# Two attentions, forward and backward, in one kernel: token-stage groups reordered, stage-edge loads and tiles moved, memory projections cut into three pieces

## The chip, the cores and the metric

The kernel runs on one core of one Trainium2 chip. The metric is device time of one execution in microseconds (us). A core has TensorE (PE in the profile; PEld is its weight load), VectorE (DVE), ScalarE (ACT), GpSimd (POOL) and SyncE (SP, which here only issues DMAs). All engines work at once, each through its own list of instructions in order, and they wait for one another by semaphores.

## The reference

A plain attention A with one shared key and value head, a recurrent attention B that carries eight memory rows from segment to segment, a gate that mixes them, and the gradients of everything with respect to the inputs and weights:

```python
def _A_ref(x, wq, wk, wv, wo):            # x 1x2048x576, 32 heads of 18, one k and one v for all heads
    q = (x @ wq).reshape(B, S, H, Dh).transpose(0, 2, 1, 3)
    k, v = x @ wk, x @ wv
    p = softmax(einsum('bhqd,bkd->bhqk', q, k) * Dh ** -0.5)
    return einsum('bhqk,bkd->bhqd', p, v).transpose(0, 2, 1, 3).reshape(B, S, H * Dh) @ wo

def _B_ref(x, mem0, Wq, Wk, Wv, Wo, seg_len):   # 32 heads of 128, segments of 32 rows, 8 memory rows
    mask = (idx[:, None] < M) | (idx[:, None] >= idx[None, :])
    mem = mem0
    for s in range(n_seg):                      # 64 segments, one after the other
        h = concatenate([mem, x[:, s * seg_len:(s + 1) * seg_len]], axis=1)
        q, k, v = (einsum('btd,dhe->bhte', h, W) for W in (Wq, Wk, Wv))
        p = softmax(where(mask, einsum('bhqe,bhke->bhqk', q, k) * scale, -1e9))
        o = einsum('bhte,hed->btd', einsum('bhqk,bhke->bhqe', p, v), Wo)
        mem = o[:, :M]
        outs.append(o[:, M:])
    return concatenate(outs, axis=1)

g = sigmoid((x * gate_w).sum(-1, keepdims=True))
out = g * _A_ref(x, ...) + (1 - g) * _B_ref(x, mem0, ...)
# returned: out, and by vjp the gradients of x, wq, wk, wv, wo, mem0, Wq, Wk, Wv, Wo, gate_w
```

All inputs and outputs are bf16.

## The kernel before

The program is a sequence of stages on one core. B is recurrent, so its forward and its backward pass are chains of small steps over the 64 segments; A is attention over 2048 x 2048 for 32 heads, a large sweep of equal steps with no dependence between them. The kernel weaves the two: a generator for a chain and a generator for a sweep are advanced in turn by `weave`, so that the sweep's matmuls fill the chain's waits.

In order of time: preparation; `b_proj` (projections of all tokens of B); `b_chain_fwd` woven with `a_pass1` (A's forward); the token stage `b_bulk`; `b_chain_bwd` woven with `a_pass2` (A's backward); `b_post` (the token gradients that the chain left over, and their product with the weights); `b_dw` (weight gradients of B, woven with the last 96 of the 1024 sweep steps of `a_pass2` and with `mem_tok`, which lays memory gradients out by tokens); `a_final`.

**Token stage, `b_bulk`.** 128 groups of (128 tokens, 4 heads) pass through a software pipeline. One turn of its loop is a tick; in each tick the list `order` names the steps and by how many ticks each lags behind the first: scores of one group, the softmax of an older one, output of one still older. `st_QT`, `st_KT`, `st_OT`, `st_VT`, `st_GT` transpose q, k, o, v and dO on TensorE into the PSUM tile `x_tr`, which has two buffers; QT and KT carry a fifth transpose along (x_dS, x_P), whose copies are `x_DT` and `x_PT`. `st_Om` and `st_Qm` open an accumulation in `x_po` (two buffers) with the whole array (memory part), `st_Ox` and `st_Qx` close it in 32 x 32 tiles (token part), and ScalarE copies it out (L740, x_o and x_dq). `B_(i)` are quarters of the output projection. `st_R` and `st_M` are softmax on VectorE and GpSimd. ScalarE also copies `x_oT` (L867) and `x_vT`.

**Woven backward chain.** `b_chain_bwd` yields 14 times in a segment, so it has 14 pieces, and between two pieces `weave` runs one step of `a_pass2`: scores `b_S` (one buffer of two banks), their exponential `b_E` on ScalarE (L1893), `b_dP`, the product `b_dS` on VectorE (L1918), and two products into `b_acc`. `lead` (12) sweep steps run ahead of the first piece, `extra` adds some after pieces 4, 7 and 9 of the first segment, and `early` (`load_WT`) asks for one twelfth of the weights WT at every fourth step, ahead of the sweep step, whose DMAs are on the same SP queue.

A segment goes, in pieces p0 to p13:

- p0, p1: `proj_part`, the gradient of the memory rows (`dm`) times `WoT`, for the two halves of the heads into PSUM tiles `r_pj` and `r_x` (one buffer each), each 5 blocks (`NKT`) of 4 matmuls, copied to `r_dOm` by ScalarE (`evac`).
- p2: `mem_T` (transposes, in r_x), copy `r_dOT` on ScalarE, `r_prod` on GpSimd, four DMAs of dOm issued by GpSimd, and the first `mem_grad` in r_pj.
- p3: `r_x` for dP, then `r_dS` on VectorE and `r_dSB` (`expand`) on GpSimd.
- p4 to p12: `heads(n)`, 48 units per segment of 4 matmuls `r_pj<-WT,r_dT`, in portions of 2, 8, 4, 4, 3, 8, 8, 6, 5; between them two more `mem_grad`, `pad_in` (GpSimd copies dS into a padded tile) and `pad_T` (VectorE transposes it, `r_dsq`), loads for the next segment, and `kv_mm(n)` in r_x with its copy and store `kv_out(n)` one piece later, which are token gradients of k and v that have nothing to do with the recurrence. `kv_first(s)` gives the numbers n0 of a segment: none in the first 4 and the last 4 segments, otherwise 3 or 4 of them.
- p13: sums of rows, the next `dm`, and a last `kv_mm`.

Sweep, chain and token gradients share the in-order lists: ScalarE holds exponentials and all copies, GpSimd holds small products and the issue of all stores, VectorE holds b_dS and the transposes.

**Stage edges.** Tiles live in pools that open and close as a stack, so a pool of one stage lies where an earlier stage had another, and its first loads wait until the old tiles are read. For the woven chain the pools are opened as rw (WoT), a3s (b_QS), a3k (b_KV), rs (the chain's tiles). `b_post` takes its tiles from rotating names of pool `sp`, `b_dw` then opens wA, whose `w_d` tiles are loaded from SP, half by plain DMAs and half by DMA transposes (L1425); `mem_tok` loads `z_src` on SP too (L588).

Of the kernel before, what the change touches and what calls it, by code (L numbers as in the profile page):

```python
# [50 lines left out]
class Kern:  # L51
# [227 lines left out]
    def weave(self, chain, sweep, lead, extra=(), early=None, n_early=0):  # L279
        steps = itertools.count()  # L280

        def step():
            i = next(steps)
            if i % 4 == 0 and i // 4 < n_early:
                early(i // 4)
            next(sweep, None)

        for _ in range(lead):
            step()
        extra = dict(extra)  # L290
        for i, _ in enumerate(chain):
            for _ in range(1 + extra.get(i, 0)):
                step()
        for _ in sweep:
            pass
# [287 lines left out]
    def mem_tok(self, wi, sp, psum):  # L583
        nc = self.nc

        def load(mt):
            src = sp.tile([P, 16, 256], BF16, name="z_src", bufs=2)
            nc.sync.dma_start(src[:], self.dTm_dram[mt][:, wi])  # L588
            return src
# [68 lines left out]
    def b_bulk(self, wp, lp, sp, psum):  # L658
# [243 lines left out]
        def st_K(t):  # L902
# [12 lines left out]
            if t % 4 == 3:  # L915
                c2 = t // 4 % 2
                for i in range(4):
# [3 lines left out]
        B_ = lambda i: lambda t: st_B(t, i)  # L921
        order = [(None, st_QT), (7, B_(0)), (None, st_KT), (7, B_(1)), (4, st_Om), (5, st_OT), (7, B_(2)), (5, st_VT),
                 (7, B_(3)), (None, st_SDm), (0, st_GT), (9, st_Qm), (2, st_R), (7, st_K),
                 (None, st_SDx), (1, st_M), (4, st_Ox), (9, st_Qx)]
        done = {st_Ox: (4,), st_VT: (5,), st_SDx: (6,), st_K: (7,), st_Qx: (9,)}
# [67 lines left out]
    def b_chain_bwd(self, wot, sp, kd, kvp, keep, psum):  # L993
# [119 lines left out]
        for s in reversed(range(NSEG)):  # L1113
# [6 lines left out]
            dOm = sp.tile([P, 8, E], BF16, name="r_dOm", bufs=1)  # L1120
            for j, nm in enumerate(("r_pj", "r_x")):
                pj = psum.tile([P, 512], F32, name=nm, bufs=1)
                self.proj_part(pj, d_, self.WoT, j, range(NKT))
                self.evac(dOm[:, 4 * j:4 * j + 4, :].rearrange("p u e -> p (u e)"), pj[:], use="s")
                if j == 1:
                    x_rows(s, 0, pT[:, 0, :])
                yield
            src = self.mem_T(dOm, psum, "r_x", 1)
# [56 lines left out]

            heads(2)
            kv_mm(n0)
            pad_in("ds", dS[:, 1, :])
            if s:
                load_a(s - 1, nxt)  # L1190
            yield
            kv_out(n0)
            heads(8)
            dSq = pad_T("ds")
            dSqB = blocks(dSq, "r_dSqB")
            x_rows(s, 1, dS[:, 0, :])
            yield
            heads(4)
            mem_cols(0, mem_grad("r_x", ((rows(L["kx"]), blk(dSB)), (rows(mrow["k"]), blk(dSB, 8)))))
            yield  # L1200
            mem_cols(1, mem_grad("r_x", ((rows(mrow["dx"]), [perm] * 8), (rows(mrow["q"]), blk(dSqB)))))
            heads(4)
            if s:
                load_b(s - 1, nxt)
            nc.gpsimd.dma_start(self.dTm_dram[s // 16][:, :, s % 16, :], dTc[:].rearrange("p w u c t -> p w (u c t)"))
            yield
            load_dT(s - 1, 2)
            heads(3)
            kv_mm(n0 + 1)
            yield  # L1210
            kv_out(n0 + 1)
            heads(8)
            if s:
# [9 lines left out]
            load_dT(s - 1, 0)  # L1223
            heads(6)
            if n1 - n0 == 4:
# [4 lines left out]
            if n1 - n0 == 4:  # L1230
                kv_out(n0 + 2)
            heads(5)
            hp = sp.tile([64, 2 * GD], F32, name="r_hp", tag="r_dSB", bufs=1)
# [38 lines left out]
    def b_post(self, sp, rp, psum, wH):  # L1272
# [5 lines left out]
        NC = NG // 2  # L1278
        pdx, C, sB, mR, T_ = {}, {}, {}, {}, {}

        def load_s(n):
# [11 lines left out]
        def load(c, names):  # L1293
# [6 lines left out]
            for w in names:  # L1300
# [5 lines left out]
                if w == "pd":  # L1306
                    d[w] = rp.tile([P, 2, 8, SEG], BF16, name="y_pd", bufs=3)
                    nc.sync.dma_start(d[w][:], self.pd_dram[tt][:, :, h0:h0 + 8, :])
                    continue
                d[w] = (rp if w == "q" else sp).tile([P, 8, P], BF16, name=f"y_{w}", bufs=3)  # L1310
                if w == "dq":
# [5 lines left out]
        def st_KV(t):  # L1317
# [13 lines left out]
            for w, pk in zip(("dk", "dv"), pks):  # L1331
                if t % 2 == 0:
                    d[w] = sp.tile([P, 8, P], BF16, name=f"y_t{w}", bufs=2)
                nc.scalar.copy(d[w][:, r, :], pk[:])
                if t % 2 == 1:
                    h0 = 8 * (t // 2 % 4)
                    nc.gpsimd.dma_start(self.xtok[w][tt * P:(tt + 1) * P, h0 * P:h0 * P + 1024],
                                      d[w][:].rearrange("p h e -> p (h e)"))

        def st_T(t):  # L1340
            d = C[t // 2]
            T_[t] = {"dq": d["dq"][:, 4 * (t % 2):4 * (t % 2) + 4, :]}
            for w in ("dk", "dv"):
                pt = psum.tile([P, 4, P], BF16, name="y_pt", bufs=2)
                for i in range(4):
                    self.tr(pt[:, i, :], d[w][:, 4 * (t % 2) + i, :], P)
                T_[t][w] = sp.tile([P, 4, P], BF16, name="y_T", bufs=5)
                nc.vector.tensor_copy(T_[t][w][:], pt[:])
            if t % 2 == 1:
                C.pop(t // 2)  # L1350
# [17 lines left out]
        stages = (st_KV, st_T, st_H)  # L1368
        dxt = [sp.tile([P, D], BF16, name=f"y_dx{i}") for i in range(2)]
        load(0, ("pd", "q", "dO"))  # L1370
# [678 lines left out]
def build_full(tc, A_x, A_wq, A_wk, A_wv, A_wo, B_mem0, B_Wq, B_Wk, B_Wv, B_Wo, gate_w, grad_out, outs_raw,  # L2049
# [10 lines left out]
    with SB("const") as cpool, tc.tile_pool(name="dram", bufs=1, space=bass.MemoryType.DRAM) as dram:  # L2060
# [18 lines left out]
        with ExitStack() as man:  # L2079
# [39 lines left out]
            k.alloc_WT(twp)  # L2119
            with SB("rw") as rw, SB("a3s") as a3s, SB("a3k") as a3k, SB("rs") as rs, \  # L2120
                    SB("rk") as rk, SB("rv") as rv, SB("rd") as rd, PS("rp") as rp, PS("a3p") as a3p:
# [88 lines left out]
```

## Time and profile before

| what | value |
|---|---|
| time, median of 3 runs | 5476.64 us (5473.39 to 5486.16) |
| profiled execution | 5478.13 us, its span 5476.4 us (1.7 us lie outside) |
| TensorE busy | 5171.7 us, 94% |
| VectorE, ScalarE, GpSimd busy | 65%, 60%, 40% |
| mean granted TensorE clock | 0.981 of full speed |
| HBM traffic | 522 MB read, 371 MB written |

| stretch of the span (us) | stage | TensorE busy | ScalarE busy | granted clock |
|---|---|---|---|---|
| 431 to 2143 | forward chain with A's forward | 1644.00 | 1360.27 | 0.99 |
| 2143 to 2783 | token stage | 576.94 | 359.04 | 0.97 |
| 2783 to 2873 | lead steps, first segment begins | 56.22 | 47.40 | 0.62 |
| 2873 to 4374 | backward chain with A's backward | 1429.58 | 1152.33 | 1.00 |
| 4392 to 4605 | b_post | 211.94 | 46.67 | 1.00 |
| 4605 to 4643 | edge to b_dw | 21.62 | 9.18 | 0.71 |
| 4643 to 5373 | b_dw | 727.64 | 156.69 | 1.00 |

How to read the profile: one execution was recorded by the hardware. A row of a timeline has start, duration, engine, source line (L740 is line 740 of the kernel), operation, output tile and input tiles, shapes, and a count where several alike follow each other; brackets give how long the engine was idle just before and which instruction or DMA released it. SPq is SP issuing DMAs. A group of the page or of the lines view adds up all such rows of one line and tile pair: busy time, mean in ns, and the idle time before them with its releasers. One group is not one limit: what ends a stage has to be read in that stage.

### The profile page before, as it was taken

What the parts mean: (1) busy time and instruction counts of PE and PEld (TensorE: products, weight loads), DVE (VectorE), ACT (ScalarE), POOL (GpSimd) and SP (SyncE); (2) the same over time, 40 slices, a digit from 0 to 9 for tenths busy, and PEclk for the clock granted to TensorE, in tenths of its full rate; (3) what the DMA queues carried; (4) which work ended last, traced back from release to release, by engine and by line L of the source; (5) the groups of instructions that cost most, each with busy time, mean ns of one, the idle gap of its engine ahead of it and who ended that gap; (6) DMA issues with size and microseconds to landing.
All of it is one profiled execution on the core that took longest, in us unless ns stands there. A gap on an engine that the chain in (4) does not pass through costs nothing. (4 is left out here: it accounts for less than half of the span.)

```text
span 5476.4 us, 221351 instructions
## 1 busy us (share of the span) xinstructions
PE 5171.7 (94%) x95713; PEld 2805.1 (51%) x95713; DVE 3579.9 (65%) x7083; ACT 3306.7 (60%) x4738; POOL 2163.2 (40%) x4186
## 2 busy tenths in 40 slices
PE   7999999999999998999979999999999998999998
PEld 6434444444444444766635555555555476754444
DVE  5337888888888887666658778888788822333322
ACT  4327787777777886655557777777777722222211
POOL 4004554555555544433324455455445411121113
PEclk9999999999999999999979999999999999999999
DMA  6645776666676555888874788888888878956553
GB/s 216 222 173 130 138 138 130 131 135 130 133 134 121 112 111 144 259 250 248 255 243 128 184 181 184 181 185 183 180 184 184 160 201 213 255 187 205 182 165 108
DMA packets 1048630, 959.14 MB, mean 175 GB/s; under 512 B 598882, under 2 KB 896747, under 8 KB 1038050
## 3 DMA queue, kind: packets, MB, share of 16 engines
q1 hardware_dynamic: 938434, 687.66, 54.2%
q0 software_dynamic: 100784, 247.24, 14.8%
q8 instruction: 748, 12.26, 1.0%
q10 hardware_dynamic: 8432, 10.08, 0.6%
q14 instruction: 232, 1.90, 0.1%
HBM read 522.08 MB, written 371.33 MB: 163 GB/s over the span
## 5 line engine op out<-in xcount | busy, mean ns | idle before, releaser
L1918 DVE TENSOR_TENSOR b_dS<-b_dP,b_E 128x512 bf16<-128x512 f32 x2048 | 1315.4, 684 | 533.5 <-PE b_dP L86 246.0
L1779 DVE TENSOR_TENSOR a_W<-a_dP,a_E 128x512 bf16<-128x512 f32 x2048 | 1315.7, 685 | 288.0 <-issue 131.3
L1893 ACT ACTIVATE b_E<-b_S 128x1024 bf16<-128x1024 f32 x1024 | 1048.8, 1024 | 605.2 <-PE b_dP L86 505.4
L1749 ACT ACTIVATE a_E<-a_S 128x1024 bf16<-128x1024 f32 x1024 | 1049.9, 1025 | 260.9 <-PE a_dP L86 173.4
L86 PEld LDWEIGHTS <-b_QS 32*128 32x128 bf16 (+1 forms) x8192 | 235.5, 89 | 564.0 <-issue 512.3
L86 PE MATMUL b_S<-b_KV,b_QS 32*128 32x512 bf16 x2048 | 408.7, 392 | 91.5 <-ACT b_E L1893 67.3
L86 PE MATMUL r_pj<-WT,r_dT 128*32 128x288 bf16 x12288 | 488.6, 289 | 6.0 <-issue 5.8
L86 PE MATMUL w_acc<-w_d,w_h 128*128 128x512 bf16 (+1 forms) x2400 | 484.6, 380 | 0.0
L86 PE MATMUL a_S<-a_QD,l_KV 32*128 32x512 bf16 x2048 | 400.6, 385 | 38.0 <-ACT a_E L1749 33.2
L86 PE MATMUL b_acc<-b_dS,b_QS 128*18 128x512 bf16 x2048 | 420.5, 392 | 3.2 <-issue 2.4
L86 PE MATMUL a_acc<-a_W,l_WK 128*32 128x512 bf16 x4096 | 413.8, 391 | 0.3 <-DVE a_W L1779 0.2
L86 PE MATMUL a_acc<-a_E,l_VK 128*32 128x512 bf16 x4096 | 404.7, 381 | 7.2 <-issue 2.7
L86 PE MATMUL b_dP<-b_KV,b_QS 32*128 32x512 bf16 x2048 | 409.2, 394 | 1.3 <-DVE b_dS L1918 1.3
L86 PE MATMUL b_acc<-b_E,b_QS 128*18 128x512 bf16 x2048 | 405.9, 392 | 2.1 <-issue 2.1
L86 PE MATMUL a_dP<-a_QD,l_KV 32*128 32x512 bf16 x2048 | 399.7, 386 | 0.5 <-issue 0.5
L86 PEld LDWEIGHTS <-r_dT 128*32 128x32 bf16 x12288 | 323.9, 97 | 101.2 <-issue 13.8
L86 PEld LDWEIGHTS <-w_h 128*128 128x128 bf16 (+1 forms) x2688 | 224.9, 100 | 257.9 <-issue 20.9
L86 PEld LDWEIGHTS <-hm 128*32 128x32 bf16 x7680 | 203.7, 97 | 195.7 <-issue 1.4
L870 POOL TENSOR_TENSOR x_prod<-x_dOT,x_oT 128x512 bf16<-128x512 bf16 x128 | 148.0, 1157 | 296.8 <-ACT x_oT L867 274.2
L86 PEld LDWEIGHTS <-l_KV 32*128 32x128 bf16 x4096 | 121.6, 91 | 250.1 <-issue 205.5
L86 PEld LDWEIGHTS <-l_WK 128*32 128x32 bf16 x4096 | 106.7, 93 | 222.0 <-issue 221.7
L86 PE MATMUL x_b<-WoN,x_oT 128*128 128x288 bf16 x1024 | 212.6, 291 | 3.2 <-issue 3.2
(465 smaller groups left out, 10106.7 us busy)
## 6 DMA issues: line engine op xcount, KB each, us to landing
b_QS<-qs_dram SPq DMA_DIRECT2D x232, 200.0 KB
dOx_dram<-p_tok SPq DMA_DIRECT2D x16, 1024.0 KB
c_vx<-vx_dram SPq DMA_DIRECT2D x64, 256.0 KB
krow_dram<-c_k POOLq DMA_DIRECT2D x64, 256.0 KB, 5.2
qrow_dram<-c_q POOLq DMA_DIRECT2D x64, 256.0 KB, 3.9
vrow_dram<-c_v POOLq DMA_DIRECT2D x64, 256.0 KB
x_q<-qx_dram SPq DMA_DIRECT2D x32, 512.0 KB
x_dO<-dOx_dram SPq DMA_DIRECT2D x32, 512.0 KB
```

Source lines behind the costliest of these rows:

```text
L86: return self.nc.tensor.matmul(out, lhsT, rhs, start=start, stop=stop, tile_position=tp, skip_group_check=True)
L870: nc.gpsimd.tensor_tensor(out=sc["prod", t][:], in0=sc["dOT", t][:], in1=oT[:], op=ALU.mult)
L1749: nc.scalar.activation(E_[n][:], S.pop(n)[:], ACT.Exp, scale=SCALEA)
L1779: nc.vector.tensor_tensor(out=W_[n][:, i, :], in0=dP[i][:], in1=E_[n][:, i, :], op=ALU.mult)
L1893: nc.scalar.activation(E_[n][:], S.pop(n)[:], ACT.Exp, scale=SCALEA)
L1918: nc.vector.tensor_tensor(out=D_[n][:, i, :], in0=dP[i][:], in1=E_[n][:, i, :], op=ALU.mult)
```

## The change

Five edits. (1) `weave` runs the sweep's step before it asks for the next weights, and the pools rs and a3s change places, so b_QS lies elsewhere and its loads are issued ahead of WT's. (2) `mem_tok` loads z_src from GpSimd's queue. (3) `b_post` allocates its tiles explicitly at its start, as rotating lists (`turn`) with the same counts, so that they lie in another order in memory. (4) The list `order` of `b_bulk` is rearranged: Om and Qm first, Ox and Qx between B_(1) and OT. (5) In `b_chain_bwd` the two projections become three pieces (4 blocks; 1 + 3 blocks with the first copy; 2 blocks with the second copy, followed by `kv_mm(n0)`, now in r_pj), `kv_out(n0)` moves to the start of the mem_T piece, the piece that held heads(2) and kv_mm(n0) disappears, `pad_in` stands directly ahead of `pad_T` in one piece, the portions of heads become 8, 4, 3, 3, 8, 8, 7, 7, and `load_a` and `load_dT(s - 1, 2)` move by one piece. A segment still has 14 pieces. The computation is the same.

```diff
--- before.py
+++ after.py
@@ -281,9 +281,9 @@
 
         def step():
             i = next(steps)
+            next(sweep, None)
             if i % 4 == 0 and i // 4 < n_early:
                 early(i // 4)
-            next(sweep, None)
 
         for _ in range(lead):
             step()
@@ -585,7 +585,7 @@
 
         def load(mt):
             src = sp.tile([P, 16, 256], BF16, name="z_src", bufs=2)
-            nc.sync.dma_start(src[:], self.dTm_dram[mt][:, wi])
+            nc.gpsimd.dma_start(src[:], self.dTm_dram[mt][:, wi])
             return src
 
         n = self.NM // P
@@ -919,9 +919,9 @@
                     due[1].append((dst[i][:, 4 * c2:4 * c2 + 4, :], dm[32 * i:32 * i + 32].rearrange("p g w e -> p g (w e)")))
 
         B_ = lambda i: lambda t: st_B(t, i)
-        order = [(None, st_QT), (7, B_(0)), (None, st_KT), (7, B_(1)), (4, st_Om), (5, st_OT), (7, B_(2)), (5, st_VT),
-                 (7, B_(3)), (None, st_SDm), (0, st_GT), (9, st_Qm), (2, st_R), (7, st_K),
-                 (None, st_SDx), (1, st_M), (4, st_Ox), (9, st_Qx)]
+        order = [(4, st_Om), (9, st_Qm), (None, st_QT), (7, B_(0)), (None, st_KT), (7, B_(1)), (4, st_Ox), (9, st_Qx),
+                 (5, st_OT), (7, B_(2)), (5, st_VT), (7, B_(3)), (None, st_SDm), (0, st_GT), (2, st_R), (7, st_K),
+                 (None, st_SDx), (1, st_M)]
         done = {st_Ox: (4,), st_VT: (5,), st_SDx: (6,), st_K: (7,), st_Qx: (9,)}
         for names in (deep, ("mT", "v", "vB", "kB")):
             load(0, names)
@@ -1118,13 +1118,20 @@
             kv_out(n0 - 1)
             nc.gpsimd.dma_start(self.dmT_dram[:, :, s, :], d_[:, 0:NKT, 0:8])
             dOm = sp.tile([P, 8, E], BF16, name="r_dOm", bufs=1)
-            for j, nm in enumerate(("r_pj", "r_x")):
-                pj = psum.tile([P, 512], F32, name=nm, bufs=1)
-                self.proj_part(pj, d_, self.WoT, j, range(NKT))
-                self.evac(dOm[:, 4 * j:4 * j + 4, :].rearrange("p u e -> p (u e)"), pj[:], use="s")
-                if j == 1:
-                    x_rows(s, 0, pT[:, 0, :])
-                yield
+            pj = [psum.tile([P, 512], F32, name=nm, bufs=1) for nm in ("r_pj", "r_x")]
+            out = lambda j: self.evac(dOm[:, 4 * j:4 * j + 4, :].rearrange("p u e -> p (u e)"), pj[j][:], use="s")
+            self.proj_part(pj[0], d_, self.WoT, 0, range(4))
+            yield
+            self.proj_part(pj[0], d_, self.WoT, 0, range(4, NKT))
+            out(0)
+            self.proj_part(pj[1], d_, self.WoT, 1, range(3))
+            yield
+            self.proj_part(pj[1], d_, self.WoT, 1, range(3, NKT))
+            out(1)
+            x_rows(s, 0, pT[:, 0, :])
+            kv_mm(n0, "r_pj")
+            yield
+            kv_out(n0)
             src = self.mem_T(dOm, psum, "r_x", 1)
             dOT = sp.tile([P, 8, 4, 8], BF16, name="r_dOT", bufs=1)
             nc.scalar.copy(dOT[:], src)
@@ -1183,32 +1190,28 @@
                                 rhs=self.WT[wi][:, h, 2 * GD * hf:2 * GD * hf + 2 * GD],
                                 start=(wi == 2 and u + cp == 0), stop=(wi == 1 and u + cp == 8), tp=(0, 32 * g))
 
-            heads(2)
-            kv_mm(n0)
+            heads(8)
             pad_in("ds", dS[:, 1, :])
-            if s:
-                load_a(s - 1, nxt)
-            yield
-            kv_out(n0)
-            heads(8)
             dSq = pad_T("ds")
             dSqB = blocks(dSq, "r_dSqB")
             x_rows(s, 1, dS[:, 0, :])
+            if s:
+                load_a(s - 1, nxt)
             yield
             heads(4)
             mem_cols(0, mem_grad("r_x", ((rows(L["kx"]), blk(dSB)), (rows(mrow["k"]), blk(dSB, 8)))))
             yield
             mem_cols(1, mem_grad("r_x", ((rows(mrow["dx"]), [perm] * 8), (rows(mrow["q"]), blk(dSqB)))))
-            heads(4)
+            heads(3)
             if s:
                 load_b(s - 1, nxt)
             nc.gpsimd.dma_start(self.dTm_dram[s // 16][:, :, s % 16, :], dTc[:].rearrange("p w u c t -> p w (u c t)"))
             yield
-            load_dT(s - 1, 2)
             heads(3)
             kv_mm(n0 + 1)
             yield
             kv_out(n0 + 1)
+            load_dT(s - 1, 2)
             heads(8)
             if s:
                 load_c(s - 1)
@@ -1221,7 +1224,7 @@
                 kv_load(0)
             yield
             load_dT(s - 1, 0)
-            heads(6)
+            heads(7)
             if n1 - n0 == 4:
                 kv_mm(n0 + 2)
             if s:
@@ -1229,7 +1232,7 @@
             yield
             if n1 - n0 == 4:
                 kv_out(n0 + 2)
-            heads(5)
+            heads(7)
             hp = sp.tile([64, 2 * GD], F32, name="r_hp", tag="r_dSB", bufs=1)
             nc.scalar.copy(hp[:], ph[64:128, :])
             nc.vector.tensor_tensor(out=hs[0:64].rearrange("p k c -> p (k c)"), in0=ph[0:64, :], in1=hp[:], op=ALU.add)
@@ -1277,6 +1280,9 @@
         NG = NTT * 8
         NC = NG // 2
         pdx, C, sB, mR, T_ = {}, {}, {}, {}, {}
+        dxt = [sp.tile([P, D], BF16, name=f"y_dx{i}") for i in range(2)]
+        turn = {w: itertools.cycle([sp.tile([P, h, P], BF16, name=f"y_{w}{i}") for i in range(n)])
+                for w, h, n in (("T", 4, 5), ("dq", 8, 3), ("tdk", 8, 2), ("tdv", 8, 2), ("dO", 8, 3))}
 
         def load_s(n):
             tt = NTT - 1 - n
@@ -1307,7 +1313,7 @@
                     d[w] = rp.tile([P, 2, 8, SEG], BF16, name="y_pd", bufs=3)
                     nc.sync.dma_start(d[w][:], self.pd_dram[tt][:, :, h0:h0 + 8, :])
                     continue
-                d[w] = (rp if w == "q" else sp).tile([P, 8, P], BF16, name=f"y_{w}", bufs=3)
+                d[w] = rp.tile([P, 8, P], BF16, name="y_q", bufs=3) if w == "q" else next(turn[w])
                 if w == "dq":
                     nc.sync.dma_start_transpose(d[w][:], self.xtok[w][tt * P:(tt + 1) * P, h0 * P:h0 * P + 1024])
                 else:
@@ -1330,7 +1336,7 @@
                 self.diag_mm(pk, d["pd"][:, x, r], d["q" if x else "dO"][:, r])
             for w, pk in zip(("dk", "dv"), pks):
                 if t % 2 == 0:
-                    d[w] = sp.tile([P, 8, P], BF16, name=f"y_t{w}", bufs=2)
+                    d[w] = next(turn["t" + w])
                 nc.scalar.copy(d[w][:, r, :], pk[:])
                 if t % 2 == 1:
                     h0 = 8 * (t // 2 % 4)
@@ -1344,7 +1350,7 @@
                 pt = psum.tile([P, 4, P], BF16, name="y_pt", bufs=2)
                 for i in range(4):
                     self.tr(pt[:, i, :], d[w][:, 4 * (t % 2) + i, :], P)
-                T_[t][w] = sp.tile([P, 4, P], BF16, name="y_T", bufs=5)
+                T_[t][w] = next(turn["T"])
                 nc.vector.tensor_copy(T_[t][w][:], pt[:])
             if t % 2 == 1:
                 C.pop(t // 2)
@@ -1366,7 +1372,6 @@
                 nc.gpsimd.dma_start(self.dxB_dram[tt * P:tt * P + n, :], dx[0:n, :])
 
         stages = (st_KV, st_T, st_H)
-        dxt = [sp.tile([P, D], BF16, name=f"y_dx{i}") for i in range(2)]
         load(0, ("pd", "q", "dO"))
         load(0, ("dq",))
         load_s(0)
@@ -2117,7 +2122,7 @@
             tw = ExitStack()
             twp = tw.enter_context(SB("tw"))
             k.alloc_WT(twp)
-            with SB("rw") as rw, SB("a3s") as a3s, SB("a3k") as a3k, SB("rs") as rs, \
+            with SB("rw") as rw, SB("rs") as rs, SB("a3k") as a3k, SB("a3s") as a3s, \
                     SB("rk") as rk, SB("rv") as rv, SB("rd") as rd, PS("rp") as rp, PS("a3p") as a3p:
                 k.weave(k.b_chain_bwd(rw, rs, rd, rv, rk, rp), k.a_pass2(a3k, a3s, a3p, 0, SWEEP, nc.sync, rv, 3), 12,
                         {4: 8, 7: 6, 9: 8}, k.load_WT, 12)
```

## Prediction

> **What bounds the kernel now.** I read the page first, then the busy time by stretch (the windows view), then the timelines engine by engine, in the one kind of stretch that each edit touches. All times are us.
>
> ```profile
> PE 5171.7 (94%) x95713; PEld 2805.1 (51%) x95713; DVE 3579.9 (65%) x7083; ACT 3306.7 (60%) x4738; POOL 2163.2 (40%) x4186
> ```
>
> TensorE is busy 94%, but the page's chain gives PE only 40% by name, so what each stage waits for has to be read there. By windows PE is busy 577 of 640 in the token stage (2143 to 2783) and 1430 of 1501 in the woven backward chain (2873 to 4374); there ACT has 1223 and DVE 1152. The largest idle stretches of PE touched by the change stand at two stage edges:
>
> ```profile
> 2792.25 0.61 PE L86 MATMUL b_S<-b_KV,b_QS 32*128 32x512 bf16 x2 [9.61 <-DMA b_QS<-qs_dram]
> ...
> 4612.99 0.61 PE L86 MATMUL b_S<-b_KV,b_QS 32*128 32x512 bf16 x2 [8.46 <-DMA b_QS<-qs_dram]
> ```
> The bracket is the idle time ahead and its releaser: query blocks that are still in flight. SP's queue around them:
>
> ```profile
> 2782.86 0.59 SPq L991 DMA_DIRECT2D WT<-st_WT  x1
> ...
> 2784.32 2.21 SPq L1879 DMA_DIRECT2D b_QS<-qs_dram  x4
> ...
> 4605.06 19.26 SPq L1425 DMA_TRANSPOSE w_d<-oh_dram  x4
> ...
> 4633.25 1.12 SPq L588 DMA_DIRECT2D z_src<-dTm_dram  x2
> ```
> At 2783 weights are asked for before queries; at 4605 transposes hold SP for 19.26 and 8.22, and z_src comes only behind them. PE then waits 3.64 (4640.73) and 1.35 (4642.48) for z_v.
>
> In the woven chain one step is one piece of b_chain_bwd and one step of the sweep. Measured from b_S start to b_S start it cannot go below 1.55: b_S, then its exponential of 1.02 on ACT, then the next b_S. Medians of the 14 steps of a segment, named by their piece from p0: 1.93, 1.73, 1.683, 1.551, 1.555, 1.632, 1.638, 1.753, 1.675, 1.631, 1.631, 1.554, 1.551, 1.574, together 23.09; the mean segment is 23.93, the 0.84 being stalls (issue) at changing places. So most steps are only 0 to 0.2 over the floor, and a wait inside a piece goes straight into the time. The rows that decide for me:
>
> ```profile
> 4036.88 0.18 PE L86 MATMUL r_pj<-perm,r_dx 128*128 128x32 bf16 x1
> ```
> (b_S of that step: 4035.92; the first gradient into r_pj starts at b_S + 0.96.)
> ```profile
> 4041.19 1.02 ACT L1893 ACTIVATE b_E<-b_S 128x1024 bf16<-128x1024 f32 x1 [0.54 <-PE b_dP L86]
> 4042.11 0.58 ACT L1103 CAST r_kvo<-r_x 128x512 bf16<-128x512 f32 x1
> ```
> (b_S: 4040.71; the copy of a kv product stands on ACT behind that step's exponential: b_S + 1.40 to + 1.98.)
> ```profile
> 4037.90 0.66 POOL L1132 TENSOR_TENSOR r_prod<-r_dOT,r_oT 128x256 bf16<-128x256 bf16 x1 [0.74 <-ACT r_dOT L1130]
> 4038.52 2.06 POOL L1135 DMA_DIRECT2D dOm_dram<-r_dOm  x4
> 4040.58 0.41 POOL L1148 COPY r_dTc<-r_dT 128x256 bf16<-128x256 bf16 x1
> 4040.93 1.08 POOL L268 TENSOR_TENSOR r_dSB<-r_dS,bmask 128x512 bf16<-128x512 bf16 x1
> 4041.96 0.23 POOL L1039 COPY r_dspad<-r_dS 128x64 bf16<-128x64 bf16 x1
> ```
> ```profile
> 4041.23 1.29 DVE L1918 TENSOR_TENSOR b_dS<-b_dP,b_E 128x512 bf16<-128x512 f32 x2 [0.27 <-issue]
> 4042.43 0.43 DVE L1043 STREAM_TRANSPOSE r_dsq<-r_dspad 128x256 bf16<-128x256 bf16 x1
> ```
> POOL works 4.3 without a pause and hands r_dspad over at 4042.19, 0.24 before DVE comes to it: no wait today, and little slack. Last, the token stage:
>
> ```profile
> 2465.64 0.60 ACT L740 CAST x_dq<-x_po 128x512 bf16<-128x512 f32 x1
> 2467.03 0.58 ACT L867 COPY x_oT<-x_tr 128x512 bf16<-128x512 bf16 x1 [0.79 <-PE x_tr L91]
> ```
> ```profile
> 2465.26 0.61 POOL L847 TENSOR_TENSOR x_P<-x_E,x_r 128x256 bf16<-128x256 bf16 x1 [0.54 <-DVE x_r L845]
> ```
> ```profile
> L91 PEld LDWEIGHTS <-x_o 128*128 128x128 bf16 x512 | 33.5, 100 | 34.8 <-DVE x_DT L754 27.7 <-issue 2.2
> L91 PEld LDWEIGHTS <-x_v 128*128 128x128 bf16 x512 | 31.6, 100 | 33.4 <-DVE x_PT L754 31.6
> ```
> The third number of the last two is idle time: both transposes wait for a bank that DVE still copies out.
>
> **Chain, per segment.** One projection of five weight blocks makes p0 1.93 and p1 1.73; the old p4 is 1.555. Spread over three pieces (0.214 per block), I get A0 0.64 + 4 x 0.214 + tail, about 1.72; A1 at the floor, 1.55; A2 with two blocks and 0.65 of kv_mm, 1.74. That is 5.01 for 5.21: -0.2. Heads (0.1215 each) stay under the floor where they grow from 5 or 6 to 7, and p7 loses one, so -0.05 at best: together -0.25. pad_in, load_dT and load_a change places at equal count; the dT loads land over a step before their heads, so zero (a late one would cost about a step, 1.5).
>
> It adds two waits. (1) kv_mm(n0) now writes r_pj, one buffer, and kv_out(n0) copies it on ACT in A3, behind that step's exponential: b_S + 1.98, by the rows. The gradient into r_pj of the same piece starts then instead of at + 0.96. Behind it on PE stands the next b_S, and behind that the whole sweep: 1.683 becomes about 2.46, +0.78. (2) pad_in and its transpose share one piece now, so from prod to the transpose there are two steps instead of three. From b_S of A3's step: kv copy 1.98, its DMA on POOL 0.6, then POOL's five rows 0.66 + 2.06 + 0.41 + 1.08 + 0.23 = 4.4, together 7.0. DVE comes to the transpose at 2.46 + 1.55 + 1.9 = 5.9 and waits 1.1; b_dS of the next step is queued behind it, and PE's b_acc waits for that. Step A7, then relieved by one head, gets +1.0 net. Bounds: nothing if POOL's DMA issue is shorter beside this load; 1.6 if none of the late b_dS is caught up.
>
> With a kv product (56 of 64 segments): -0.25 + 0.78 + 1.0 = 1.55, times 56 = 87. Without (8): -0.25 + 1.0 = 0.75, 6. Some of the 0.84 of stalls falls into the new waits: 2 steps of 14, 0.12, off 64 times, -8. Sum **+85**, bounds 35 and 120.
>
> **Token stage, 128 ticks of 4.81 mean.** Om to OT takes 0.306 for 0.213 of work, OT to VT 0.62 for 0.478; with Ox and Qx ahead of OT those waits go: -0.24 a tick. Switching once more between whole-array and 32-row tiles costs 0.096 (x_po on x_kmB to x_po on x_k 0.309 for 0.213). New: GT's bank is freed by the oT copy, which now stands on ACT behind the copies of o and dq. From Ox's start: 0.45 + 0.48 + 0.48 + 0.58 = 2.0 against 1.84 of PE work: +0.17 to 0.21. And KT's transposed x_P: today from GT (2463.79) to x_P done (2465.87) is 2.08; the new order has about 1.85 of PE work in between on even ticks, more on odd ones where K lies there: +0.1 mean. Sum +0.12 x 128 = **+15**; -25 if both new waits are hidden, +45 if both are paid in full.
>
> **Edges.** b_QS asked for before WT, in memory that is free already: of the 9.6, DMA landing remains about 2. But the twelve lead steps then end near 2807, and the first projection needs WoT (issued 2793.30 on POOL, which waits for the last stores, landed about 2808.5): **-7**, 6 to 9.6. The clock there is granted at 0.62 from 2783 to 2873, and b_S takes 0.61 instead of 0.39. The Trainium skill, "TensorE: Matmul & The Clock Gate", Part 1, says that TensorE falls to half clock after an idle window of about 3.4 us and needs about as much busy time to return; by that rule closing the gap would save some 2 us more. The trace speaks for little of it: b_S still takes 0.61 in the later lead steps, PE being busy 56 of these 90 us.
>
> At 4605 the tiles of b_post that are read to the end no longer lie under the first w_d, so these loads start some 9 earlier and b_QS (issued 4605.20 on ACT) meets less traffic: -4 (0 to 5). z_src goes to POOL, which is idle there, past SP's transposes: the 5.0 of waits for z_v go. Sum **-9**, 5 to 11. The Trainium skill, "DMA: Bandwidth & Descriptors", on issuing engines, sends plain copies to SP or ACT rather than GpSimd, which speaks against this move; by it z_src would lose some tenths of a us. The 27 us of transposes ahead of it on SP outweigh that. The rotating tiles inside b_post cost nothing: PE is dense there (largest wait 0.59 for y_dO), each buffer count is kept.
>
> **Sum.** 85 + 15 - 7 - 9 = +84 on the profiled execution (5478.1, span 5476.4), which is 1.5 above the median: 5562 there, **5560** as a median. A measurement tells about 0.2% (11 us) from no change.
>
> **Rivals.**
> - Only the r_pj wait appears, DVE's does not (POOL's dOm issue, 2.06 for four, shorter). For: the slack is sensitive to 1 us. Against: POOL ran these rows back to back. 56 x (0.78 - 0.25) - 4 = +26, +15 - 16: 5503. Chance 0.20.
> - Faster: copies do not hold the banks, above all because the kv copy gets in front of the exponential. ACT's queue is in order, so this needs kv_out to be issued first; the row at 4042.11 speaks against it. Then -0.25 x 64 = -16 chain, -16 edges, -15 for half of the token gain: 5430 to 5465, about 5445. The change gains as soon as both chain waits cost under about 0.5 a segment with the token stage at zero (0.25 + 16/64), under 0.75 with its half gain. Chance 0.15.
> - The edits do not do what they say: first queries wait for WoT anyway, z_src for its source, tiles do not matter: 85 + 15: 5576, inside the first case's range.
>
> **Numbers.** Both waits: 0.61 (with the last rival 0.65), own range 5520 to 5605. For 8 in 10 I reach down over the middle case: 5482 to 5604, leaving out the faster case and the tails. Faster 0.15, same 0.03, slower 0.82.
>
> **What would show it.** In the changed profile: steps A0 to A2 at 1.72, 1.55, 1.74; the gradient into r_pj released by ACT r_kvo at b_S + 2.0; r_dsq on DVE released by POOL r_dspad, with b_acc waiting for b_dS afterwards; mean segment 25.3 for 23.93. In the token stage PE waits for ACT x_oT ahead of x_dO and for POOL x_P, none ahead of x_o and x_v; tick 4.93. At the edges 2 to 3 instead of 9.6, and no z_v wait. Wrong if r_kvo does not release r_pj, or if the chain's segments stay at 23.9 or below.

## The result, and the profile after

The changed kernel takes 5696.87 us (median of 4 runs, 5682.04 to 5701.26) against 5475.02 us for the kernel before in the same comparison: ratio 1.0403, 95% interval 1.037 to 1.0435. It is slower, as forecast, but by 217 us (spans 5693.3 against 5476.4) where the prediction had 84, and outside its range of 5482 to 5604.

The two profiled executions, cut at the same events:

| stretch | before | after | difference | forecast |
|---|---|---|---|---|
| start to last a_W (end of the forward chain) | 2142.8 | 2140.4 | -2.4 | 0 |
| to the last x_po (token stage) | 639.9 | 651.1 | +11.3 | +15 |
| to the first b_S | 9.6 | -0.1 | -9.7 | -7 (counted at the chain's end) |
| to the last b_S of the weave (928 steps) | 1591.5 | 1681.8 | +90.3 | +85 |
| to the last y_pdx (b_post) | 220.8 | 347.1 | **+126.3** | 0 |
| to the end (edge, b_dw, a_final) | 871.9 | 873.1 | +1.2 | -9 |

Of the 133 us that the prediction misses, 126 lie in one row, b_post, which it had set to nothing; 10 more lie in the last row. The page's busy line of the changed kernel:

```profile
PE 5283.8 (93%) x95713; PEld 2836.8 (50%) x95713; DVE 3586.9 (63%) x7083; ACT 3310.1 (58%) x4738; POOL 2169.4 (38%) x4198
```

PE has the same 95713 instructions and 112 us more busy time: part of the loss is instructions that each take longer. (The windows view gives 64 of the 112 for the woven chain, 34 for b_post.) The windows view of b_post alone, first of the kernel before, then of the changed one (stretch, length, busy time of PE, PEld, DVE, ACT, POOL, granted clock, DMA share, GB/s):

```profile
4391.60:4604.53 212.93, 212.34 (x3154) 168.22 (x3152) 39.25 (x109) 46.23 (x85) 30.78 (x55) 1.00 0.75 197
```
```profile
4497.00:4820.25 323.25, 245.85 (x3154) 181.66 (x3151) 39.27 (x109) 46.14 (x85) 30.78 (x55) 0.85 0.50 132
```

The same 3154 matmuls: 77 us of waiting have come in, and at a granted clock of 0.85 the matmuls themselves take 34 us more. A first wait of 14.62 stands just ahead of the stretch shown; with it the 126 us are 92 of waiting and 34 of slower matmuls. Who waits for what is in the changed kernel's PE and SP timelines:

```profile
4495.18 2.10 PE L86 MATMUL y_pdx<-WT,y_dq 128*128 128x288 bf16 x8 [14.62 <-DMA y_dq<-dqx_dram]
...
4583.84 2.10 PE L86 MATMUL y_pdx<-WT,y_dq 128*128 128x288 bf16 x8 [11.89 <-DMA y_dq<-dqx_dram]
...
4590.77 1.14 PE L86 MATMUL y_pdx<-WT,y_dq 128*128 128x288 bf16 x8
```
```profile
4566.85 0.54 SPq L1314 DMA_DIRECT2D y_pd<-pd_dram  x1
...
4579.13 1.29 SPq L1318 DMA_TRANSPOSE y_dq<-dqx_dram  x1
```

At 4571.9 PE has all of H's older inputs, yet stands still until a y_dq load that SP issues only at 4579.13, behind a dozen loads of y_sB and y_mR, has landed. SP itself had been held at y_pd until PE reached that tick. Each of the 24 chunks has two y_pdx groups that read y_dq, in two ticks that follow each other, and for 18 chunks the first of the two waits so: 92.0 us in the wait list, 77.4 of them in the stretch shown above (changed kernel's lines view of it):

```profile
L86 PE MATMUL y_pdx<-WT,y_dq 128*128 128x288 bf16 x378 | 68.6, 336 | 77.4 <-DMA y_dq<-dqx_dram 77.4
```

The reason is in the program order. `load(t // 2 + 2, ("dq",))` stands between st_T and st_H of an even tick t. With three tiles, the tile that it takes is the one of chunk t/2 - 1, which st_H(t - 2) reads right behind the load in the same tick, and st_H(t - 1) in the next. In the kernel before, `sp.tile(...)` handed out a new instance, and SP waited for the old one's last reader (in the wait list of before SP L1312 waits for PE y_pdx 65.2 us in 16 times; nobody else was held up). With tiles that are allocated once, the load is simply the latest write ahead of st_H(t - 2): now PE's product waits for the load, and reads what it brought, dq of chunk t/2 + 2. So in the changed kernel and in post_only below, 21 of the 24 chunks are multiplied with the dq of the chunk three further on, and "The computation is the same", in the section on the change, does not hold for edit (3). The matmuls are the same in number and shape, so the times can still be compared. The same list of SP instructions, the same counts of tiles; only the direction of one dependence has turned round.

The chain shows what was forecast, in one segment of the changed kernel (PE, ACT, DVE, POOL, PE; b_S of A3's step at 4111.44):

```profile
4113.47 0.18 PE L86 MATMUL r_pj<-perm,r_dx 128*128 128x32 bf16 x1 [1.01 <-ACT r_kvo L1103]
```
```profile
4111.92 1.02 ACT L1898 ACTIVATE b_E<-b_S 128x1024 bf16<-128x1024 f32 x1 [0.24 <-ACT r_dOm L83]
4112.84 0.58 ACT L1103 CAST r_kvo<-r_pj 128x512 bf16<-128x512 f32 x1
```
```profile
4118.61 0.45 DVE L1043 STREAM_TRANSPOSE r_dsq<-r_dspad 128x256 bf16<-128x256 bf16 x1 [1.30 <-POOL r_dspad L1039]
```
```profile
4118.35 0.23 POOL L1039 COPY r_dspad<-r_dS 128x64 bf16<-128x64 bf16 x1
```
```profile
4119.81 0.37 PE L86 MATMUL b_dP<-b_KV,b_QS 32*128 32x512 bf16 x1 [0.48 <-DVE b_dS L1923]
```

The gradient into r_pj starts at b_S + 2.03 (before: + 0.96; forecast: + 2.0). DVE waits 1.30 for POOL (forecast 1.1). This is one segment of many alike: in the 56 with a kv product A3 is about 2.5, and on DVE 63 of the 64 transposes wait for r_dspad, 1.29 in the median. Medians of the 14 steps A0 to A13 are 1.816, 1.554, 1.742, 2.514, 1.554, 1.844, 1.802, 1.868, 1.675, 1.631, 1.631, 1.554, 1.552, 1.63; the mean segment is 25.30 for 23.93. The medians of A5 and A7 describe no segment: DVE's wait lengthens either A5 (over 2.0 in 30 segments) or A7 (over 2.5 in 31), never both.

In the token stage the waits for DVE's copies ahead of x_o and x_v are gone, and idle time ahead of x_dO (25.1 for 4.8) and a wait for x_P (36.8 for 10.6) have come. The profile names POOL x_P, but for x_dO no releaser ("issue"): that this is ACT's x_oT copy, as the prediction has it, is left to bulk_ot_first below (changed kernel, lines view, idle time of the weight loads):

```profile
L91 PEld LDWEIGHTS <-x_v 128*128 128x128 bf16 x512 | 38.7, 99 | 7.9 <-DVE x_PT L754 0.5
...
L91 PEld LDWEIGHTS <-x_dO 128*128 128x128 bf16 x512 | 38.6, 98 | 25.1 <-issue 24.1 <-DMA x_vmB<-vm_dram 0.9
...
L91 PEld LDWEIGHTS <-x_P 128*128 128x128 bf16 x128 | 12.3, 96 | 36.8 <-POOL x_P L847 35.7
```

And at the edge to b_dw:

```profile
4824.85 0.60 PE L86 MATMUL b_S<-b_KV,b_QS 32*128 32x512 bf16 x2 [4.61 <-DMA b_QS<-qs_dram]
```

4.61 for 8.46, with no wait for z_v right behind it. Waits for z_v come later in the stage instead, 2.6 us at 5048 and 3.3 at 5240, 5.9 together for 5.0 before.

### The profile page after: what moved, and what is told of

Read it like the earlier page. It is cut to its first block, busy times and chain, and to the rows that moved or that the text cites. A ratio compares the mean times of both kernels' runs of the same rounds, so it can differ in the third digit from the quotient of the medians.

```text
span 5693.3 us, 221407 instructions
## 1 busy us (share of the span) xinstructions
PE 5283.8 (93%) x95713; PEld 2836.8 (50%) x95713; DVE 3586.9 (63%) x7083; ACT 3310.1 (58%) x4738; POOL 2169.4 (38%) x4198
## 4 chain that ended last, share of the span: by engine, by line
PE 42%; DMA 5%; POOL 4%; ACT 4%; issue 4%; DVE 2%; SPq 2%; ACTq 0%; POOLq 0%; DVEq 0%
PE w_acc L86 11%; PE r_pj L86 8%; PE b_S L86 5%; PE b_acc L86 5%; PE r_x L86 4%; PE y_pdx L86 2%; DMA y_dq<-dqx_dram 2%; ACT b_E L1898 2%; PE x_tr L91 1%; PE x_po L86 1%; ACT x_oT L867 1%; PE f_big L86 1%; POOL dOm_dram L1142 1%; PE x_b L86 1%; POOL x_P L847 1%
## 5 line engine op out<-in xcount | busy, mean ns | idle before, releaser
L86 PE MATMUL b_dP<-b_KV,b_QS 32*128 32x512 bf16 x2048 | 429.4, 402 | 16.6 <-DVE b_dS L1923 16.6
L86 PE MATMUL b_acc<-b_dS,b_QS 128*18 128x512 bf16 x2048 | 444.2, 401 | 0.3 <-issue 0.3
```

The source lines that it names most:

```text
L86: return self.nc.tensor.matmul(out, lhsT, rhs, start=start, stop=stop, tile_position=tp, skip_group_check=True)
```

## The experiments

Ratios are against the kernel before, run beside them, each with its 95% interval. The kernel before took 5443 to 5475 us in these comparisons, so ratios are compared across them and not times. The first question was where the 126 us of b_post come from, and whether the five edits add up; then which wait in the chain costs what.

**post_only.** Only the `turn` lists of b_post.

```diff
-                d[w] = (rp if w == "q" else sp).tile([P, 8, P], BF16, name=f"y_{w}", bufs=3)
+                d[w] = rp.tile([P, 8, P], BF16, name="y_q", bufs=3) if w == "q" else next(turn[w])
...
```

> The kernel before with the rotating tiles of b_post alone. Theory: the reload of a y_dq tile now stands ahead of that tile's last reader in program order, so the product y_pdx waits for the transposing load that was issued just ahead of it, instead of the load waiting for the product; b_post takes 344 us as in the changed kernel, not 218, and the time is 5475 + 126 - 4 = about 5597 us (1.022 of before). (The product takes a later chunk's dq here, as it does in the changed kernel; its time is to be read so.) Rival: b_post is slow only because the chain's pools ahead of it lie elsewhere and its first loads come late; then this run stays within 15 us of before.

Measured: 1.022 (1.0186 to 1.0254), 1.022 expected. The row of b_post, cut as in the table above, is 350.2 us. In this run:

```profile
4393.00:4713.70 320.70, 243.58 (x3139) 180.18 (x3137) 39.26 (x109) 46.16 (x85) 30.77 (x55) 0.85 0.49 130
```

The same as in the changed kernel, although the chain ahead of it is the old one. The rival falls.

**after_dq_late.** The changed kernel, with the dq load behind the last reader:

```diff
-                if n == 1 and t % 2 == 0 and t >= 2:
+                if n == 2 and t % 2 == 1 and t >= 3:
                     load(t // 2 + 2, ("dq",))
```

> The changed kernel with one edit: the load of dq stands one tick later, behind the last product that reads the old tile; tiles and their places stay. Theory: b_post returns to 218 us, with SP waiting for PE y_pdx ahead of each y_dq as in the kernel before; 5697 - 126 = about 5571 us (1.0175 of before). Rival (the place of the tiles in memory costs the time): no change, about 5697 us.

Measured: 1.0205 (1.0179 to 1.023). The row of b_post is 221.4 us for 347.1 in the changed kernel:

```profile
4483.20:4696.50 213.30, 212.34 (x3154) 168.19 (x3152) 39.24 (x109) 46.17 (x86) 30.79 (x55) 1.00 0.82 213
```

PE's busy time is back at 212.34 to the hundredth, at full clock, with the tiles still where the change put them. (SP's waits are now listed at y_pd, 53.6 us in 14 times, not at y_dq as expected; nobody on PE waits for them.) So the place of the tiles costs nothing; the order of load and reader does. One moved load is worth 126 us of b_post, 1.0403 to 1.0205 in the ratio, and what is left of the change is +2.05%, near the +1.5% of the prediction.

**chain_only.** Only the edits of `b_chain_bwd`.

> The kernel before with the edits of b_chain_bwd alone. Theory of the prediction, both new waits: first to last b_S of the chain 1592 + 90 = 1682 us, mean segment 25.3, the time 5565 us (1.0165). Rival, only the r_pj wait: mean segment about 24.4, 5503 us (1.005).

Measured: 1.0162 (1.0129 to 1.0195), mean segment 25.29. Both waits are there.

**chain_kvout_early.** chain_only with

```diff
             kv_mm(n0, "r_pj")
+            kv_out(n0)
             yield
-            kv_out(n0)
```

> The kernel with the chain's edits alone, and kv_out(n0) ahead of the yield, so that its copy stands on ACT ahead of the step's exponential. Theory (the r_pj wait is ACT's order): A3 falls from 2.51 to about 1.7 while A2 grows by 0.2 because the exponential starts later; -0.6 x 56 = -34 us, 1.010 of before. Rival (A3 is long because of mem_T's own wait for r_dOm, or of DVE): A3 stays at 2.5, 1.016.

Measured: 1.0067 (1.0045 to 1.009), more than forecast. A3 falls from 2.514 to 1.704 and A2 stays at 1.742. ACT's timeline of this kernel (b_S of the step: 4021.19; the first gradient into r_pj: 4022.06, so + 0.87):

```profile
4020.85 0.58 ACT L83 CAST r_dOm<-r_x 128x512 bf16<-128x512 f32 x1
4021.31 0.61 ACT L1103 CAST r_kvo<-r_pj 128x512 bf16<-128x512 f32 x1
4021.80 1.05 ACT L1896 ACTIVATE b_E<-b_S 128x1024 bf16<-128x1024 f32 x1
```

The copy now runs mostly where ACT would have waited for b_S anyway. The exponential starts at b_S + 0.61 instead of + 0.48, and A3, 1.704 for 1.683 in the kernel before, shows next to nothing of it.

**chain_pad_early.** chain_only with `pad_in("ds", ...)` ahead of `self.expand(dSB...)` instead of behind heads(8).

> The kernel with the chain's edits alone, and pad_in of dS ahead of the expansion into r_dSB on GpSimd, so r_dspad is there 1.08 us earlier. Theory (DVE waits for POOL's row behind four DMAs and r_dSB): A5 to A7, together 6.2 in the mean, fall to 5.3; -0.9 x 64 = -58 us, 1.0055 of before. Rival (the length of A5 to A7 is the 8 heads and r_dSB itself): no change or longer by 0.2 a segment, 1.016 to 1.019.

Measured: 1.0113 (1.0093 to 1.0133). DVE's wait falls from 1.30 to

```profile
4080.72 0.45 DVE L1043 STREAM_TRANSPOSE r_dsq<-r_dspad 128x256 bf16<-128x256 bf16 x1 [0.28 <-POOL r_dspad L1039]
```

and A5 to A7 from 6.2 to 5.65 in the mean. This is half the expected gain. With A3's wait cured as well (chain_both, next) A5 to A7 are 5.26, so part of the rest comes from A3's wait; another part is A6 (1.97 for 1.80), which now has r_dSB later. That A3's wait acts by pushing back r_kvo's DMA on POOL was not tested. The mechanism stands; the price of this wait was set too high, that of the other too low.

**chain_both.** Both cures together.

> Both of the two cures of the chain's edits together. Theory: -34 and -58 add, what is left is the gain of the three pieces, -0.25 x 64 = -16 us against before: 0.997 to 1.000. Rival (the two waits hide each other): less than the sum, 1.003 or more.

Measured: 0.9992 (0.9982 to 1.0002), mean segment 23.71. The two waits explain the whole loss of the chain: A3 is 1.705, A5 to A7 5.26. What the three pieces themselves gain is hardly measurable: A0 is 1.82, not 1.72, so p0, p1 and p4, together 5.21, became 5.11; A6 keeps 0.3 of lateness, and A13, with seven heads for five, is 1.63 for 1.574.

**weave_only.** Sweep step ahead of the weights, and the pools' order.

> The kernel before with the sweep's step ahead of the weights' request and the pools in their new order, alone. Theory: the 9.6 us ahead of the first b_S close to 0 to 2, but the first projection waits for WoT and starts only some 0 to 3 us earlier, the end by 0 to 7 us: 0.9987 to 1.000 of before. Rival (the whole gap is gained): -9.6 us, 0.998.

Measured: 0.9999 (0.9986 to 1.0012). The gap of 9.6 is closed, but PE now waits for the first projection's weights and then for r_dx (weave_only's PE timeline):

```profile
2796.95 1.47 PE L86 MATMUL r_pj<-WoT,dm 128*32 128x512 bf16 x12 [1.14 <-DVE dm L1006]
2798.79 0.62 PE L86 MATMUL r_pj<-WoT,dm 128*32 128x512 bf16 x4 [0.36 <-DMA WoT<-st_WoT]
2800.95 0.62 PE L86 MATMUL r_pj<-WoTt,dm 128*32 128x512 bf16 x4 [1.55 <-DMA WoTt<-st_WoTt]
...
2808.67 0.21 PE L86 MATMUL r_pj<-perm,r_dx 128*128 128x32 bf16 x1 [2.05 <-DMA r_dx<-dmx_dram]
```

WoT is issued 10.7 us after the end of the token stage, as before. Counted from that end, the 14th sweep step starts 5.6 us earlier than before, the 16th 1.7, the 48th 0.1 later. The gain is given back inside the first segments: the waits for WoT and WoTt are 1.9 of it, the one for r_dx 2.05, and 1.75 is lost between the first two b_S. Steps 17 to 20 also take 1.77 for 1.55, their b_S 0.61 as in the lead steps where the kernel before has 0.39.

**bulk_only.** Only the order of b_bulk.

> The kernel before with the new order of b_bulk alone. Theory: tick 4.91 instead of 4.81, +12 us, 5487 us (1.002). Rival, that the longer token stage in the changed kernel is chance (stalls at changing places): within 4 us of before.

Measured: 1.0038 (1.0022 to 1.0054), about 20 us (12 to 29), near the +15 and within its bounds. The token stage takes 621.5 to 642.2 us in the ten profiles with the old order and 650.4 to 658.0 in the three with the new one, 16 us more in the mean: the rival, chance, falls, and one pair alone (+11.3) says little. Median distances between PE groups in undisturbed ticks: the waits at OT and VT are down by 0.27, the new wait at GT (x_SD to x_dO) is 0.359 for 0.113, every tick, and x_k to x_P is 0.544 for 0.223 on ticks without K. Added up over a tick the medians give 4.60 for 4.37. Of these 0.23 the mean tick shows only 0.1 in the profiled pair of before and after (4.93 for 4.82). Where the rest is hidden was not looked into.

**bulk_ot_first.** The new order, but OT and B_(2) ahead of Ox and Qx.

> The kernel with the new order of b_bulk alone, but OT and B_(2) ahead of Ox and Qx, so that the copy of oT stands on ACT ahead of those of o and dq. Theory: GT's wait of 0.245 a tick goes, P's wait on ticks without K (0.32) shrinks as GT comes earlier against nothing, OT waits for its bank again by about 0.1: tick 4.75 to 4.8, 0.999 to 1.001 of before (1.0038 with the order as changed). Rival (the wait at GT is not the oT copy): GT's gap stays 0.36 and the ratio 1.004.

Measured: 1.0051 (1.0033 to 1.0069), slower still. Half of the theory holds: GT's gap is back at 0.113, so the oT copy behind o and dq on ACT is what GT waited for. The other half was wrong: OT waits again for its bank, in the median for 0.3 instead of 0.1. The DVE copy of x_DT, which frees it, is late by then; Om no longer lies between KT and OT:

```profile
2467.86 0.40 PE L91 MATMUL x_tr<-identB,x_o 128*128 128x128 bf16 x4 [0.24 <-DVE x_DT L754]
```

Each of the three orders tried pays somewhere for the two buffers of x_tr; the order before pays least.

**post_late, zsrc_only, best.** The tiles of b_post with the late load, z_src on GpSimd's queue, and both of these with chain_both.

> The kernel before with the rotating tiles of b_post and the load of dq one tick later, alone. Theory: b_post takes its 213 us again, with the first w_d loads asked for earlier, so that the wait for b_QS at the edge falls from 8.5 to about 4.6; -4 us, 0.9993 of before. Rival (the earlier w_d loads push something later): 1.000 to 1.001.

> The kernel before with z_src loaded from GpSimd's queue, alone. Theory: the two waits for z_v, 5.0 us together, go; 0.9991 of before. Rival: a transfer that is late behind SP's transposes takes their place (o_T, for which the changed kernel waits 6.3 us), 1.000.

> The kernel before with the three pieces and both cures of chain_both, the tiles of b_post with the late load of dq, and z_src on GpSimd's queue; weave and b_bulk as before. Theory: the single gains add: -4 (chain) -4 (edge) -5 (z_v) us, 0.9975 of before. Rival (gains at the edge are eaten by the next transfer): 0.999.

Measured: post_late 0.9984 (0.9974 to 0.9995), with the wait for b_QS at the edge at 4.54 and no wait for z_v above 0.3 us in its whole trace, although z_src is still on SP there; zsrc_only 0.9992 (0.9979 to 1.0006), which cannot be told from no change; best 0.9986 (0.9975 to 0.9998). In zsrc_only the two waits at the edge are gone, one of 1.4 for w_d has come, and the waits for z_v stand 216 and 408 us behind the edge's first b_S, 5.9 us in the sum for 5.0. The last of them in zsrc_only's PE and POOL timelines:

```profile
5003.32 1.23 POOL L588 DMA_DIRECT2D z_src<-dTm_dram  x2
...
5011.73 2.42 POOL L599 COPY z_v<-z_src 128x2048 bf16<-128x2048 bf16 x1 [4.21 <-DMA z_src<-dTm_dram]
```
```profile
5012.46 0.40 PE L91 MATMUL z_pt<-identB,z_v 128*128 128x128 bf16 x4 [2.18 <-DVE z_v L599]
5014.21 0.61 PE L91 MATMUL z_pt<-identB,z_v 128*128 128x128 bf16 x4 [1.36 <-POOL z_v L599]
```

The load is issued at 5003.32, behind stores in GpSimd's list, one of which had to wait 3.99 for its source, and z_v waits for it. So the move of z_src has put its waits off, while the new place of b_post's tiles alone leaves none in post_late. These waits vary from profile to profile with an unchanged edge too (5.0 before, 5.6 in chain_only, 1.4 in weave_only). best, which has the move, waits 6.2 for z_v, as late as zsrc_only. best is faster than the kernel before by some 0.14%, no more than post_late. Whether its chain gains anything on top of post_late is within the intervals and stays open.

The parts add up: 0.38% (bulk_only), 1.62% (chain_only), 2.2% (post_only), 0 (weave_only) and -0.08% (zsrc_only) are 4.1%, with intervals of 0.1 to 0.3 each; the change measures 4.03%.

## Why the prediction was right or wrong

- **The step that failed:** "The rotating tiles inside b_post cost nothing: PE is dense there ..., each buffer count is kept." The counts were kept and the conclusion did not follow. What had to be compared is which instruction comes first in the program, the load into a tile or the last read of it. With 126 us instead of 0 it is larger than all other terms together. It was to be seen without the chip, in the order of `load` and the stages and in before's own profile: SP's 65.2 us of waits for y_pdx say that these loads were issued ahead of their tile's last reader. None of the prediction's rivals had it either.
- **Chain, +85:** measured +90.3 between the first and the last b_S, mean segment 25.30 (25.3 forecast). The r_pj wait came as worked out from the rows at 4036.88 and 4042.11 (A3 2.514, forecast 2.46). DVE's wait came too (1.30, forecast 1.1), in A5 in about half of the segments and in A7 in the others; the three steps A5 to A7 together are longer by 1.0, as summed. The gain of -0.25 was too large: A0 is 1.82, not 1.72, and the heads save nothing. Two slips in the working matter little: -0.25 + 0.78 + 1.0 is 1.53, not 1.55 (1 us in the sum), and where it says that ACT has 1223 and DVE 1152 in the chain it is the other way round.
- **Rivals of the chain:** "only the r_pj wait" falls by chain_only and chain_pad_early. The faster rival's condition, kv_out in front of the exponential, is what chain_kvout_early makes true, and there it frees 0.95% of the time (1.0162 to 1.0067), as the mechanism said.
- **Token stage, +15:** +11.3 in the pair of profiles, +16 in the mean of all, about +20 (12 to 29) by bulk_only. Both new waits are there; GT's is 0.245 (0.17 to 0.21 forecast), x_P's 0.32 on every second tick (0.1 mean forecast, 0.16 measured). The size was right within what these runs can tell; that the pair's tick is 4.93, as forecast to the hundredth, is in part luck, since the same old order gave token stages 20 us apart.
- **Edges, -7 and -9:** two local waits went as forecast (9.6 closed, 8.46 to 4.61), but weave_only gains nothing by its 48th step. The prediction named WoT and took 2.6 off the 9.6 for it; the waits for it are 1.9, and the wait for r_dx, the longer first step and the slower ones, which it did not name, take most of the rest. At the second edge the tiles' new place gives -8.8 by post_late (-3 to -14), where the z_v waits went and the one for b_QS halved; the prediction gave it -4. The step that failed there is "the 5.0 of waits for z_v go": moved to POOL's list they come later, as 5.9. In the changed kernel's own trace the stretch behind b_post is no shorter (+1.2), a wait of 6.3 for o_T being another part.

## What to carry to other kernels

When tiles of a rotating pool are replaced by tiles that are allocated once, compare, for each load, its place in the program with the last read of the tile that it overwrites: a load issued ahead of that read was held back by the pool's new instance, and with a fixed tile the reader waits for the load instead, and reads it. A copy that frees a bank has to be issued ahead of the long instruction on its in-order engine, not behind it: one moved line was worth 0.95% here. A load that is moved to another engine's list stands behind what that list holds: look along the whole stage, not only at the wait that it was to cure. A closed gap at the beginning of a stage is a gain only if the next resource that the stage needs comes earlier too.

## What the runs showed of the hardware

Waits of 2 to 3 us are paid twice. In the changed kernel eight y_pdx took 2.10 us after a wait of 14.62 and after one of 11.89, and 1.14 in a tick without a wait. They took 2.10 also after a wait of 3.32 (at 4598.85), and after this one:

```profile
4612.34 2.10 PE L86 MATMUL y_pdx<-WT,y_dq 128*128 128x288 bf16 x8 [2.47 <-DMA y_dq<-dqx_dram]
```

In the first 2 us of the groups at 4495.18, 4583.84 and 4612.34 the granted clock is 0.50 (windows view). The length of the wait does not settle it: after 3.11 (at 4546.29) eight took 1.52, after 2.20 (at 4757.36) 1.15. Over b_post the granted clock was 0.85, and of the 110 us that PE's stretch of b_post grew, 34 are matmuls that ran slower. The Trainium skill, "TensorE: Matmul & The Clock Gate", Part 1, gives an idle window of about 3.4 us after which TensorE drops to half its clock until it has been busy for about as long. The half clock agrees with this trace (0.50, and 2.10 against 1.14); as the shortest wait that costs something the 3.4 us do not, since 2.47 was enough.

In the woven chain the granted clock falls with a shorter wait: from its first to its last b_S the granted clock is 0.95 in the changed kernel, chain_only and chain_pad_early, where PE waits about 1.0 for r_kvo in 54 or 55 segments, and 0.98 in the kernel before, chain_kvout_early and chain_both, where it does not.
